# Attention with a soft mixture of experts on one core: the opening's roundings and duplicates reordered, logits spread ahead of the experts, extra constant products late

## Chip, core and metric

The kernel runs on one core of a Trainium2 chip. The core has five engines with a queue of their own each: PE (matrix products, into PSUM), DVE (vector), ACT (scalar functions and copies), POOL (general purpose) and SP, which here only issues transfers (DMA). Engines wait for each other by semaphores; each executes its own queue in order. The metric is the device time of one execution in microseconds.

## The reference

```python
def _attn_ref(q, k, v, f):            # q, k, v: 8 x 8 x 576 x 64; f: 8 x 8 x 576
    scale = 1.0 / np.sqrt(D)
    scores = scale * np.matmul(q, k.transpose(0, 1, 3, 2))
    cum = np.cumsum(np.log(np.clip(f, 0.0001, 1.0)), axis=-1)
    decay = cum[:, :, :, None] - cum[:, :, None, :]
    scores = np.where(causal, -1000000000.0, scores + decay)
    scores = scores - np.max(scores, axis=-1, keepdims=True)
    attn = np.exp(scores)
    attn = attn / (np.sum(attn, axis=-1, keepdims=True) + 1e-09)
    return np.matmul(attn, v)

def _moe_ref(x, phi, w1, w2):         # x: 4608 x 512; phi: 512 x 32; 8 experts, 4 slots each
    logits = x @ phi
    d = softmax over tokens of logits;  slot_input = d.T @ x
    for e in range(E):
        slot_out[e] = np.maximum(slot_input[e] @ w1[e], 0.0) @ w2[e]
    c = softmax over slots of logits
    return c @ slot_out
```

The attention's output, with heads side by side, is the x of the mixture.

## The kernel before

The 64 (batch, head) pairs are treated as 32 head pairs g, heads i = 2g and 2g + 1. For each head PE runs three stages. `s1` (L230) computes rough scores, whose row maxima DVE takes in `tops` (L243). PE turns these maxima (`mturn`, L253), ACT rounds them into a row (`mrows`, L262) and a transfer puts it into YA as one more contraction row. `s2` (L280, L281) computes the scores again, transposed and exactly, with the decay and minus the maximum in extra rows; the two products use the rounded operands WA, YA and a second pair WB, YB, which hold a duplicate of the rounded half and the difference that rounding left. ACT takes the exponential (`expo`, L287) into PTS, POOL zeroes the non-causal part (`causal`, L295, L298), and `s3` (L313) multiplies with the values V. DVE divides (`norm`, L328 to L333).

Operands are made as follows. `load_qk` loads a pair into one of three buffers RAW; `round_k` (L183) and `round_q` (L188) round it on ACT into WA and YA, a head at a time; `dup_k` (L199) and `dup_q` (L203) copy that by transfer into WB and YB; `low_k` (L209) and `low_q` (L214) subtract on POOL, which needs the duplicate (for k) or the rounded half (for q). `load_cum` brings the decay rows. All transfers are issued by SP, in program order.

The loop over g from 1 to 31 is a software pipeline: iteration g does `s2` and `s3` of pair g, `s1` of heads 2g + 3 and 2g + 4, and the roundings of pair g + 3. What comes ahead of it (pair 0, and the start of pairs 1 and 2) is written out by hand at L530 to L688 and is called the opening here. There the decay is made from f: logarithm (L558), prefix sum (L562), rounding (L571), rounding error (L572, L573); three copies on ACT (L583, L584) and transfers (L580) put these rows into WA[0] and WA[1]. The constant rows of WA and YA of the buffers 1 and 2 come from a small buffer `fill` by transfers (L575, L576). `warm` (L527) issues products of constants whose result nobody reads.

The order of everything is the order of the program; no scheduler moves instructions.

From iteration 5 on the mixture joins: logits (L387), a running maximum over tokens (`mgroup`, `mtop`, `mcast`), exponentials (`weigh2`), their transposes (`tokens`, L457, L458) and the sum over tokens (`dispatch`, L490). The logits of a batch come as 128 whole columns and 16 more for the last 64 tokens, which `spread` (L402) puts into a masked form LX with the help of `own_j` (L671, L672). After iteration 31 comes a tail (L858 to L910) for the last batch, with transposes of the combine weights (`cols`, L712) between its steps. Then the experts run from the list `STEPS`: first products (`mlp1`, L932), scaling and maximum with zero (`relu`, L940, L942), transposes of the hidden rows (`own`, L952, with copies at L955) and second products (`mlp2`, L969), with weights that are streamed (L128) into every buffer that has become free. The output blocks (L1047) are copied (L1049) and stored (L1051).

## Time and profile before

| | |
|---|---|
| time, three runs | 390.32, 390.36 and 391.53 us; median 390.36 us |
| the profiled execution's own time | 391.48 us |
| its span, first to last instruction | 389.8 us |
| mean granted clock of PE | 0.982 |
| busiest engines | PE 95%, DVE 76%, ACT 69%, POOL 65% of the span |
| start of `s2` of head 0, 2, 4, 6, 8 | 13.57, 26.82, 36.89, 45.66, 54.43 us |
| last weight transfer issued; first output issued | 351.6; 360.85 us |

A row of the order in time reads: start in us, duration in us, engine, line of the kernel, operation, what is written and read with its shape, count, and in brackets how long the engine idled before it and what ended that. A row of a stretch reads: from and to in us, its length, then busy time and instructions of PE, PE's weight loads, DVE, ACT and POOL, the clock granted to PE (1.00 is full), the mean busy share of the DMA engines and GB/s. A row of the chain reads: start, duration, what the end of the program waited for at that time.

### The profile page before, as it was taken

The numbers are of one execution on the slowest core, as the hardware profiler recorded it, in microseconds if no ns is written. First come the engines' busy times: TensorE is split into PE (matmuls) and PEld (weight loads), VectorE is DVE, ScalarE is ACT, GpSimd is POOL, SyncE is SP. The second block draws the span as 40 slices with busy tenths as digits, with TensorE's granted clock in tenths as the row PEclk, the third lists the DMA queues.
The fourth block names the chain that finished last, engine by engine and source line by source line (L and its number), as shares of the span: only waits on it lengthen the run. The fifth ranks groups of instructions, "written<-read, shape, count | busy, mean of one in ns | idle before, by whom it ended". The sixth has DMA issues, their size and how long they took to land.

```text
span 389.8 us, 15241 instructions
## 1 busy us (share of the span) xinstructions
PE 370.1 (95%) x5881; PEld 327.9 (84%) x5881; DVE 297.5 (76%) x1161; ACT 269.9 (69%) x685; POOL 251.6 (65%) x339
## 2 busy tenths in 40 slices
PE   8989999999999999999999999999999999999950
PEld 7879999999999999999999999999999986444630
DVE  7788887989798979897988898889988743412651
ACT  8887787878787878788878787878776553010540
POOL 3769987878787878787878787878787620000000
PEclk9999999999999999999999999999999998999995
DMA  6866667777867787777777777767765999999898
GB/s 206 230 153 161 172 189 208 200 199 243 243 197 224 216 236 218 218 209 216 215 211 215 215 213 213 220 208 220 211 183 159 309 341 385 409 408 373 270 358 345
DMA packets 34120, 93.72 MB, mean 240 GB/s; under 512 B 4234, under 2 KB 10048, under 8 KB 34048
## 3 DMA queue, kind: packets, MB, share of 16 engines
q1 hardware_dynamic: 34048, 92.75, 76.2%
q8 instruction: 46, 0.75, 0.8%
q14 instruction: 26, 0.21, 0.1%
HBM read 63.93 MB, written 9.73 MB: 189 GB/s over the span
## 4 chain that ended last, share of the span: by engine, by line
PE 79%; DMA 11%; POOL 3%; ACT 3%; DVE 2%; issue 1%; DVEq 0%; SPq 0%; ACTq 0%; POOLq 0%
PE pv L313 25%; PE ring L280 14%; PE ring L281 12%; PE s L230 11%; DMA w<-in_w 7%; PE pv L340 4%; PE lg L387 2%; PE ds L490 2%; POOL YB L214 1%; DMA out<-p 1%; DMA RAW<-in_qk 1%; PE pv L969 1%; PE ring L490 1%; ACT PTS L287 1%; DMA out<-RAW 1%
## 5 line engine op out<-in xcount | busy, mean ns | idle before, releaser
L287 ACT ACTIVATE PTS<-ring 128x320 f32<-128x320 f32 (+2 forms) x256 | 118.1, 502 | 50.2 <-PE ring L281 39.8
L243 DVE CUSTOM_DVE_ANT_0 s<-s,mask 128x320 f32<-128x320 f32 (+4 forms) x320 | 138.5, 452 | 6.1 <-PE s L230 1.0
L280 PE MATMUL ring<-YA,WA 67*128 67x320 f32 (+9 forms) x384 | 119.5, 325 | 0.0
L281 PE MATMUL ring<-YB,WB 128*128 128x320 f32 (+4 forms) x384 | 110.7, 296 | 0.0
L313 PE MATMUL pv<-V,PTS 128*64 128x65 f32 x3200 | 101.9, 223 | 0.9 <-POOL PTS L295 0.5
L209 POOL TENSOR_TENSOR WB<-RAW,WB 64x576 fp32r<-64x576 f32 x64 | 91.0, 1423 | 15.9 <-DMA YA<-V 5.3
L313 PEld LDWEIGHTS pv<-V,PTS 128*64 128x64 f32 x3200 | 97.1, 138 | 4.7 <-issue 1.2
L230 PE MATMUL s<-WA,YA 66*128 66x288 f32 (+9 forms) x384 | 100.4, 317 | 0.4 <-DVE MT L243 0.3
L214 POOL TENSOR_TENSOR YB<-RAW,YA 64x576 fp32r<-64x576 f32 x64 | 89.7, 1420 | 2.5
L280 PEld LDWEIGHTS ring<-YA,WA 67*128 67x128 f32 (+3 forms) x384 | 68.9, 181 | 5.3 <-issue 1.6
L281 PEld LDWEIGHTS ring<-YB,WB 128*128 128x128 f32 (+1 forms) x384 | 69.9, 182 | 0.0
L230 PEld LDWEIGHTS s<-WA,YA 66*128 66x128 f32 (+1 forms) x384 | 63.0, 191 | 5.3 <-DVE MT L243 0.5
L243 DVE DVE_READ_ACCUMULATOR2_ANT MT<- 128x1 f32 x372 | 52.7, 142 | 0.0
L298 POOL TENSOR_SCALAR_AFFINE_SELECT PTS<-PTS 128x128 f32<-128x128 f32 (+1 forms) x128 | 31.3, 265 | 29.9 <-ACT PTS L287 26.4
L295 POOL TENSOR_SCALAR_AFFINE_SELECT PTS<-PTS 128x384 f32<-128x384 f32 x64 | 33.3, 520 | 18.2 <-ACT PTS L287 14.1
L183 ACT CAST WA<-RAW 64x576 fp32r<-64x576 f32 x64 | 40.0, 669 | 4.0 <-DMA RAW<-in_qk 3.4
L340 PE MATMUL pv<-cs,X 128*128 128x128 f32 x155 | 42.1, 273 | 0.6 <-DVE X L333 0.6
L188 ACT CAST YA<-RAW 64x576 fp32r<-64x576 f32 x64 | 40.0, 669 | 0.4
L243 DVE CUSTOM_DVE_ANT_0 s<-s,mask,MT 128x288 f32<-128x288 f32 x62 | 32.6, 526 | 9.6 <-PE s L230 1.0
L333 DVE TENSOR_TENSOR X<-pv,rl 128x320 f32<-128x320 f32 (+1 forms) x65 | 31.5, 486 | 2.4 <-DMA V<-in_v 0.3
L376 ACT COPY XTS<-pv 128x128 f32<-128x128 f32 (+1 forms) x93 | 25.3, 307 | 1.1 <-PE pv L340 0.8
L340 PEld LDWEIGHTS pv<-cs,X 128*128 128x128 f32 x155 | 21.9, 142 | 1.5 <-DVE X L333 0.9
(215 smaller groups left out, 376.5 us busy)
## 6 DMA issues: line engine op xcount, KB each, us to landing
w<-in_w SPq DMA_DIRECT2D x44, 512.0 KB
RAW<-in_qk SPq DMA_DIRECT2D x31, 576.0 KB
V<-in_v SPq DMA_DIRECT2D x32, 325.0 KB
WB<-WA SPq DMA_DIRECT2D x31, 288.0 KB
YB<-YA SPq DMA_DIRECT2D x31, 288.0 KB
p<-in_w SPq DMA_DIRECT2D x7, 512.0 KB
out<-RAW SPq DMA_DIRECT2D x12, 256.0 KB
out<-p SPq DMA_DIRECT2D x5, 512.0 KB
```

Source lines behind the costliest of these rows:

```text
L183: nc.scalar.copy(WA[g % 3][0:64, S * h : S * h + S], RAW[g % 3][64:128, h])
L188: nc.scalar.copy(YA[g % 3][0:64, h, 64:640], RAW[g % 3][0:64, h])
L209: nc.gpsimd.tensor_tensor(t[0:64], RAW[g % 3][64:128, h], t[64:128].bitcast(F32), op=ALU.subtract)
L214: nc.gpsimd.tensor_tensor(YB[g % 2][64:128, h], RAW[g % 3][0:64, h], YA[g % 3][0:64, h, 64:640].bitcast(F32), op=ALU.subtract)
L230: nc.tensor.matmul(t[:, o : o + w], ya[0:m, h, 128 * blk : 128 * blk + 128], wa[0:m, j0 : j0 + w], start=True, stop=True)
L243: nc.vector.tensor_tensor_reduce(out=t[:, o : o + w], in0=t[:, o : o + w], in1=mask[:, m0 : m0 + w], scale=1.0, scalar=top if n == 3 else ...
L280: nc.tensor.matmul(o, wa[0:m, j0 : j0 + n], ya[0:m, h, 64 + i0 : 64 + i0 + w], start=True, stop=False)
L281: nc.tensor.matmul(o, wb[:, j0 : j0 + n], yb[:, h, i0 : i0 + w], start=False, stop=True)
L287: nc.scalar.activation(PT[i % 2][:, SEG_O[bank] : SEG_O[bank] + at], t[:, 0:at], AF.Exp, scale=0.125)
L295: nc.gpsimd.affine_select(d3, d3, pattern=[[0, 3], [1, 128]], compare_op=ALU.is_ge, fill=0.0, base=0, channel_multiplier=-1)
L313: nc.tensor.matmul(pvv[h][64 * u : 64 * u + 64, t, :], PT[h][:, at : at + 64], V[:, g % 2, c, 65 * h : 65 * h + 65], start=(c == 0), stop= ...
L340: nc.tensor.transpose(pm[:, 0:128], x[:, t, 128 * (p % 2) : 128 * (p % 2) + 128], ident)
```

## The change

Four things are changed.

1. The opening. The duplicates of pair 1 and 2 are issued by head, and their roundings come earlier or later, by head too. Two of the three ACT copies of decay rows become transfers, and the fill transfers are spread differently over the queue. The fill buffer lies in XTS instead of V. Score products of heads 1 to 4 (`first`) are moved among the values products and into iteration 1. Three warm products fewer are issued.
2. `own_j` is computed at the end of iteration 2 instead of in the opening.
3. In the tail five warm products of 64 or 128 columns are added, into a free part of the buffer pv[0].
4. In the experts, the logits of the last batch are copied and spread ahead of the first product instead of after the second expert's, and the last `own` is called one step earlier.

```diff
+    def fills(m, n):
+        if n == 0:
+            nc.sync.dma_start(WA[m][66:67].bitcast(F32), fill[0:1, 0 : 2 * S].bitcast(F32))
+        else:
+            nc.sync.dma_start(YA[m][64:66].rearrange("c h s -> c (h s)").bitcast(F32), fill[32:34].bitcast(F32))
+
     nc.vector.tensor_copy(fp[lane, 0:S], fz)
+    nc.sync.dma_start(WA[0][64:65, S:].bitcast(F32), fp[96:97, 0:S].bitcast(F32))
+    dup_k(0, 1, 2)
+    fills(1, 0)
...
-    for h in range(2):
-        nc.scalar.copy(WA[0][64:65, S * h : S * h + S], fp[64 + 32 * h : 65 + 32 * h, 0:S])
-    nc.scalar.copy(WA[0][96:97, S:], fp[96:97, S:])
+    nc.sync.dma_start(WA[0][96:97, S:].bitcast(F32), fp[96:97, S:].bitcast(F32))
...
+    fills(1, 1)
+    nc.scalar.copy(WA[0][64:65, 0:S], fp[64:65, 0:S])
     round_q(0, 1)
-    nc.scalar.activation(fin[:, 0:1], ones[:, 0:1], AF.Exp)
     dup_q(0, 1, 2)
...
     round_k(1, 0)
+    round_q(1, 0)
+    dup_k(1, 0, 1)
+    dup_q(1, 0, 1)
...
+    round_k(1, 1)
+    first(1, 3, WARM[1])
     both(0, 0)
-    first(1, 3)
+    first(2, 0)
     both(0, 1)
+    round_q(1, 1)
+    dup_k(1, 1, 2)
+    dup_q(1, 1, 2)
...
-    round_q(2)
-    first(3, 2)
-    first(3, 3)
+    round_k(2, 0)
+    round_q(2, 0)
+    dup_q(2, 0, 1)
+    dup_k(2, 0, 1)
     causal(1)
-    low_q(2)
     low_k(3)
     low_q(3)
-    nc.vector.tensor_reduce(own_j[:, 0], ident.rearrange("p (j s) -> p j s", j=4), axis=AX.X, op=ALU.add)
-    nc.vector.tensor_scalar(own_j[:, 1], own_j[:, 0], 1.0e30, -1.0e30, op0=ALU.mult, op1=ALU.add)
-    s3(0, alone[0])
+    s3(0, alone[0][:13])
+    first(3, 2)
+    s3(0, alone[0][13:])
+    first(3, 3)
+    s3(0, alone[1][:13])
     first(4, 0)
+    s3(0, alone[1][13:])
     mturn(1, 1, 2)
     mrows(1, 1, 2)
-    dup_q(2)
-    dup_k(2)
+    round_k(2, 1)
+    round_q(2, 1)
+    dup_q(2, 1, 2)
+    dup_k(2, 1, 2)
     first(4, 1)
...
-    round_k(3)
-    round_q(3)
...
         expo(h0, 2)
+        if g == 1:
+            round_k(3, 0)
+            round_q(3, 0)
...
+    warm(2, cs, 128, late=True)
     nc.vector.tensor_reduce(mb[:, 2:3], EX[:, 0:192], axis=AX.X, op=ALU.add)
...
     nc.vector.tensor_scalar_mul(mk, mk, fin[:, 2:3])
+    weigh(b)
+    spread(b, 0)
...
-        if (e, k) in ((2, 0), (4, 0), (6, 0), (5, 4)):
-            own({2: 0, 4: 2, 6: 4, 5: 6}[e])
+        if (e, k) in ((2, 0), (4, 0), (6, 0), (4, 4)):
+            own({(2, 0): 0, (4, 0): 2, (6, 0): 4, (4, 4): 6}[e, k])
         if (e, k) == (1, 0):
-            weigh(b)
-            spread(b, 0)
             tokens(b, 0)
             combine(b, 0)
```

The numbers behind names in the next rows are buffer numbers: RAW_95, RAW_96 and RAW_97 hold pairs 0, 1 and 2 (RAW_95 then pair 3), WA_86, YA_85, WB_88 and YB_87 belong to pair 1, WA_94 and YA_93 to pair 2.

SP's queue, from the load of pair 2 to the maxima row of head 2, before:

```order
L203 DMA YB_91<-YA_89 64x576
L174 DMA RAW_97<-in_qk 128x1152
L178 DMA V<-in_v 128x650
L174 DMA RAW_95<-in_qk 128x1152
L199 DMA WB_88<-WA_86 64x1152
L203 DMA YB_87<-YA_85 64x2x576
L194 DMA WA_94<-cumd 2x2x576
L265 DMA YA_85<-mr_0_337 1x5x128
```

and with the change:

```order
L174 DMA RAW_97<-in_qk 128x1152
L178 DMA V<-in_v 128x650
L199 DMA WB_88<-WA_86 64x576
L203 DMA YB_87<-YA_85 64x576
L199 DMA WB_88<-WA_86 64x576
L203 DMA YB_87<-YA_85 64x576
L194 DMA WA_94<-cumd 2x2x576
L265 DMA YA_85<-mr_0_336 1x5x128
L174 DMA RAW_95<-in_qk 128x1152
```

The duplicates of pair 1 are cut in two and stand ahead of the load of pair 3, which moves behind the maxima row.

ACT's queue from the first maxima row of pair 1 into iteration 1, before:

```order
L262 CAST mr_0_337<-pv_147 5x128
L183 CAST WA_94<-RAW_97 64x576 x2
L287 ACTIVATE PTS<-ring_150 128x320
L287 ACTIVATE PTS<-ring_151 128x512
L188 CAST YA_93<-RAW_97 64x576 x2
L262 CAST mr_1_408<-pv_148 5x128
L183 CAST WA_90<-RAW_95 64x576 x2
L188 CAST YA_89<-RAW_95 64x576 x2
L287 ACTIVATE PTS<-ring_149 128x448
L287 ACTIVATE PTS<-ring_150 128x320
L287 ACTIVATE PTS<-ring_151 128x320
```

and with the change, from the second maxima row on:

```order
L262 CAST mr_1_430<-pv_148 5x128
L183 CAST WA_94<-RAW_97 64x576
L188 CAST YA_93<-RAW_97 64x576
L287 ACTIVATE PTS<-ring_149 128x448
L287 ACTIVATE PTS<-ring_150 128x320
L287 ACTIVATE PTS<-ring_151 128x320
L183 CAST WA_90<-RAW_95 64x576
L188 CAST YA_89<-RAW_95 64x576
L376 COPY XTS<-pv_147 128x128 x2
L287 ACTIVATE PTS<-ring_149 128x512
L287 ACTIVATE PTS<-ring_150 128x448
L183 CAST WA_90<-RAW_95 64x576
```

Two roundings of pair 2 and all four of pair 3 now stand behind the second maxima row, those of pair 3 among the exponentials of iteration 1.

POOL's queue around the selection of head 1, the stretch that iteration 1 waits for, before:

```order
L209 TENSOR_TENSOR WB_88<-RAW_96,WB_88 64x576
L295 AFFINE_SELECT PTS<-PTS 128x3x128
L298 AFFINE_SELECT PTS<-PTS 128x128
L298 AFFINE_SELECT PTS<-PTS 128x64
L214 TENSOR_TENSOR YB_87<-RAW_96,YA_85 64x576
```

and with the change:

```order
L209 TENSOR_TENSOR WB_88<-RAW_96,WB_88 64x576
L214 TENSOR_TENSOR YB_87<-RAW_96,YA_85 64x576
L295 AFFINE_SELECT PTS<-PTS 128x3x128
L298 AFFINE_SELECT PTS<-PTS 128x128
L298 AFFINE_SELECT PTS<-PTS 128x64
```

The selection of head 1 moves behind the second subtraction of head 2.

In the tail the five warm products stand on PE behind the first two transposes of `cols`, ahead of the products of `mcast`, ahead of `tokens`, and two behind it:

```diff
     next(c0)
+    warm(1, cs, 64, late=True)
     mgroup(b)
...
     next(c0)
+    warm(1, cs, 64, late=True)
     mcast(b)
...
     next(c1)
+    warm(1, cs, 128, late=True)
     tokens(b, 1)
+    warm(2, cs, 128, late=True)
```

## Prediction

> **What bounds the kernel now.** I read the page first, then the chain of waits over the opening, then the stretches, then the opening and the end in order of time.

> ```profile
> span 389.8 us, 15241 instructions
> PE 370.1 (95%) x5881; PEld 327.9 (84%) x5881; DVE 297.5 (76%) x1161; ACT 269.9 (69%) x685; POOL 251.6 (65%) x339
> ...
> 34.42 0.53 POOL PTS L295
> 34.95 0.04 issue
> 35.00 1.96 PE pv L313 x58
> 36.96 0.40 PE ring L280
> ...
> 40.00:50.00 10.00, 9.97 (x152) 9.44 (x151) 8.36 (x36) 8.47 (x22) 8.51 (x13) 1.00 0.64 186
> ```

> PE is the engine of the long middle: from 40 to 50 us it is busy 9.97 of 10. What moves the start of that middle moves the end by as much. The first 37 us are different: in the chain PE's values product (L313) waits for POOL's causal selection (L295). Why POOL is late, the rows in order of time say:

> ```profile
> 5.81 0.52 SPq L199 DMA_DIRECT2D WB<-WA  x1
> 9.83 1.41 POOL L209 TENSOR_TENSOR WB<-RAW,WB 64x576 fp32r<-64x576 f32 x1 [5.31 <-DMA YA<-V]
> 17.26 0.67 ACT L183 CAST WA<-RAW 64x576 fp32r<-64x576 f32 x1
> 17.95 0.67 ACT L188 CAST YA<-RAW 64x576 fp32r<-64x576 f32 x1
> 17.96 0.48 SPq L199 DMA_DIRECT2D WB<-WA  x1
> 22.16 1.40 POOL L209 TENSOR_TENSOR WB<-RAW,WB 64x576 fp32r<-64x576 f32 x1 [5.12 <-DMA YB<-YA]
> 24.68 1.41 POOL L214 TENSOR_TENSOR YB<-RAW,YA 64x576 fp32r<-64x576 f32 x1
> ```

> The second pair's rounding ends on ACT at 17.9, its duplicate (both heads in one transfer) is issued at 17.96, and POOL's subtraction for head 2 starts at 22.16, after 5.12 us of idling: 4.2 us from issue to use. (The row names another buffer's transfer; the subtraction reads WB.) From 22.16 on POOL runs without a gap up to the selection of 34.42. So the opening costs PE whatever POOL is late.

> **The opening, step by step.** Roundings of both operands of head 2 move ahead of the first maxima on ACT, and the duplicate goes by head. The SP queue now fixes its time. Ahead of the first V load stand two issues more than before (the rows that ACT copied, now transfers):

> ```profile
> 7.10 0.59 SPq L575 DMA_DIRECT2D WA<-V  x1
> 13.88 0.33 SPq L178 DMA_DIRECT2D V<-in_v  x1
> ```

> An issue of this kind takes 0.59, so V goes out between 13.88 (if the queue's waits absorb the two) and 15.1; the duplicate of head 2 follows 0.33 later, 14.2 to 15.4. I take 15.0. It runs behind the same kind of load as before, so the 4.2 from issue to use stays: POOL starts at T = 19.2 instead of 22.16. Bounds: 14.2 + 4.0 (the first duplicate: issued 5.81, used 9.83) = 18.2, and 15.4 + 4.2 + 0.8 (more data ahead: both loads) = 20.4.

> POOL gains 3.0, but not all of it reaches PE, since the order behind it changes too. The selection of head 1 now stands behind both subtractions of head 2: 1.40 + 1.41 + 0.53 and issue gaps, so T + 3.45 = 22.65. Behind it PE has the values of head 1 in two halves with a score product between, then the turn of head 3's maxima (L253), and only then ACT's L262 can start. ACT is in order, and behind that L262 now stand six roundings that were done earlier or beside waits:

> ```profile
> 23.79 0.25 ACT L262 CAST mr<-pv 5x128 fp32r<-5x128 f32 x1 [0.17 <-PE pv L253]
> 25.97 0.92 PE L313 MATMUL pv<-V,PTS 128*64 128x65 f32 x24
> 27.53 1.31 ACT L287 ACTIVATE PTS<-ring 128x448 f32<-128x448 f32 x3 [0.95 <-PE ring L281]
> 29.68 0.43 ACT L376 COPY XTS<-pv 128x128 f32<-128x128 f32 x2 [0.84 <-PE pv L340]
> 30.75 1.03 ACT L287 ACTIVATE PTS<-ring 128x512 f32<-128x512 f32 x2 [0.64 <-PE ring L281]
> 31.67 0.38 ACT L376 COPY XTS<-pv 128x256 f32<-128x256 f32 x1
> 31.92 0.44 ACT L349 COPY XTS<-pv 64x64 f32<-64x64 f32 x2
> 32.38 0.77 ACT L287 ACTIVATE PTS<-ring 128x320 f32<-128x320 f32 x2
> 33.41 0.60 ACT L287 ACTIVATE PTS<-ring 128x512 f32<-128x512 f32 x1
> ```

> PE: two halves at about 0.8 (24 records took 0.92 with their latency), 0.5 for score product and turn: L262 at T + 5.6 = 24.8. Before, ACT waited 0.95 + 0.84 + 0.64 in this stretch; now it does not wait. Its work up to the last exponential of head 3: L262 twice 0.5, six roundings at 0.69 (17.26 to 17.95) 4.1, exponentials 1.31 + 1.03 + 0.77 + 0.60 = 3.7, copies 0.43 + 0.69 (31.67 to 32.36) = 1.1; sum 9.4, so ACT ends it at 34.2 (before: 34.01, the same place). PE's values are then half done, instead of waiting for POOL; about 23 of 50 products need that last exponential. At the pace of the row (58 records in 1.96) their 46 records take 1.55. The next score stage (before: 36.96 less its latency, 36.89) starts at 35.8. **Opening: 1.1 us earlier.** With T at 18.2 it is 2.1, at 20.4 nothing.

> Costs taken as nothing, and what covers them:

> ```profile
> 10.38 0.53 PE L230 MATMUL s<-WA,YA 97*128 97x320 f32 x2
> 11.62 0.53 DVE L243 CUSTOM_DVE_ANT_0 s<-s,mask 128x320 f32<-128x320 f32 x1
> 44.67 0.17 DVE L328 TENSOR_SCALAR rl<-pv 128x5 f32<-128x5 f32 x1 [0.82 <-PE pv L313]
> 22.65 0.94 DVE L672 TENSOR_SCALAR own_j<-own_j 128x4 f32<-128x4 f32 x1
> ```

> Head 1's decay rows now come by transfer; its first product ran at 10.38, and DVE reaches it at 11.62, so the rows may be 0.9 later for free, and 1:1 beyond. The own_j pair (0.94 and some 0.3) goes to the end of iteration 2, into DVE's 0.82 of waiting there; 0.4 remains, which the next iteration's wait takes up. Three warm products fewer in the opening fill waits only. The fill in XTS instead of V has the same shape.

> **The end.** After the last attention PE's clock is halved for a while, and PE waits at three places:

> ```profile
> 324.00:326.00 2.00, 1.73 (x36) 1.73 (x40) 1.32 (x5) 0.52 (x2) 0.00 (x0) 0.59 1.02 381
> 326.00:328.00 2.00, 2.00 (x18) 1.05 (x10) 0.64 (x2) 0.37 (x1) 0.56 (x2) 0.55 1.02 418
> 360.00:362.00 2.00, 2.00 (x32) 1.28 (x32) 0.88 (x3) 0.81 (x3) 0.00 (x0) 1.00 0.11 45
> ...
> 11.21 1.10 PE L527 MATMUL pv<-cs 128*128 128x184 f32 x6
> 318.50 0.84 PE L490 MATMUL ring<-X,LD 128*32 128x128 f32 x24
> 319.96 0.64 PE L490 MATMUL ring<-X,LD 128*32 128x128 f32 x16
> 324.27 2.32 PE L490 MATMUL ring<-X,LD 128*32 128x128 f32 x40 [0.42 <-DVE LD L464]
> 332.93 0.41 PE L458 MATMUL ring<-cs,LGM 128*128 128x32 f32 x2 [0.62 <-DVE LGM L402]
> 355.60 1.93 PE L969 MATMUL ring<-w,X 128*32 128x256 f32 x32 [0.35 <-DVE X L955]
> 360.85 4.22 SPq L1051 DMA_DIRECT2D out<-RAW  x6
> ```

> Between these PE runs gapless, and the first output leaves at 360.85; the DMA share of 0.11 in 360 to 362 says that the transfers then wait for PE, not for weights. So PE's gains here count, up to the 1.8 us that DMA idles there.

> The spread ahead of the experts removes the wait of 0.62, and the earlier own(6) the 0.35: **minus 0.97**. Late is next: the same products, without a wait. The five late products are fp32 of 64 to 128 columns. Three calls of 184 took 1.10; by columns (512 in all) five cost 1.0, at a full 0.37 each 1.85. The last two lie in the 0.42 that PE waits for LD; the others stand on the chain of maximum, broadcast and exponential. **Plus 0.6** (up to 1.4).

> They can pay by the clock. Forty products took 2.32 at the halved clock; 24 and 16 took 0.84 and 0.64 at the full one: 0.84 lost there, and with the transposes behind about 1.1. The profiled execution took 391.48 us by its own time (389.8 span and 1.7 around it); the runs shown took 390.32, 390.36 and 391.53. Two values, 1.1 apart: I read it as this drop, present in some executions and absent in others, so the median of 390.36 holds none. [...]

> **The sum**, against the profiled execution: 391.48 − 1.1 (opening) − 0.97 (two waits) + 0.6 (late products) − 1.1 (clock kept) = 388.8; with the rounding of the terms 388.9. Against the median that is 1.5 less, since the median has the clock's 1.1 already.

> **Rivals.**
> *The clock still drops.* For it: the window before the drop was already filled to nine tenths by the profile's count, and five short products add little. Then 388.9 + 1.1 = 390.0. [...]
> *The opening gives nothing.* ACT has no reserve in my chain; 1.1 us of waits there (PE behind DVE's maxima) eat it. 388.9 + 1.1 = 390.0.
> *The opening gives all of POOL's 3.0.* If PE and ACT reach their places early enough, T decides: 388.9 − 1.9 = 387.0. Against it: ACT's sum.
> *Slower: the duplicate lands no earlier.* It is cut in two but stands behind two loads. In the new order PE's next stage stands at T + 16.6, so the opening loses from T = 20.3 on. At the old T of 22.2 it starts at 38.8: 391.48 + 1.9 − 0.97 + 0.6 − 1.1 = 391.9. Against it: it is issued some 3 us sooner.

> **How the numbers follow.** Forecast 0.43; clock drops 0.20; opening nothing 0.16; all of POOL 0.13; slower 0.08. The range takes in all but the slower one: 387.0 to 390.3 (390.0 and a little for the dearer late products). 0.3%, about what a measurement of this kernel can tell from no change, is 1.17 us: the borders are 389.19 and 391.53. Of the forecast's 0.43, some 0.35 lies under 389.19 (T up to 19.5); with the 0.13 and 0.01 of the clock's case that makes faster 0.49. Slower is its 0.08 and 0.01 of the second rival; the rest, 0.42, is the same.

> **What would show it.** POOL's subtraction for head 2 near 19.2 and not 22.16. ACT gapless from L262 of head 3 to the last exponential of head 3. The score stage of pair 2 at 35.8. No PE wait ahead of L458 and between the experts' second products; first output 0.4 earlier relative to the last attention product, and 1.5 where the clock holds. A granted clock of 1.00 in the stretch after the late products. It would be wrong first where T or ACT's sum is.

## The result: slower by 0.9%

| | before | changed |
|---|---|---|
| median (lowest to highest) | 390.94 us (390.32 to 400.96, 4 runs) | 394.47 us (393.99 to 395.13, 4 runs) |
| profiled execution, own time and span | 391.48, 389.8 us | 393.99, 392.3 us |
| start of the score stage of head 4 (first L280) | 36.89 us | 40.76 us |
| from the start of the last values product to the end of the span | 75.2 us | 73.7 us |

The ratio is 1.0086, interval 1.0061 to 1.0111: slower, where 388.9 and a range up to 390.3 were predicted. The 400.96 is an execution in a slower state, which the ratio leaves out; the other three have a median of 390.36. The last two rows of the table divide the loss. The opening gives head 4 to PE 3.9 us later, the middle passes that on, and the end wins 1.5 back: 3.9 − 1.5 = 2.4, as the two profiled executions differ (393.99 − 391.48 = 2.5). The end is as predicted (1.47); the opening is 5.0 later than the 35.8 of the prediction.

The page of the changed kernel begins:

```profile
span 392.3 us, 15255 instructions
PE 370.3 (94%) x5885; PEld 327.6 (84%) x5885; DVE 297.3 (76%) x1161; ACT 268.9 (69%) x683; POOL 252.2 (64%) x339
```

PE's busy time is the same as before (370.1), so nothing costly was added: in sum PE waits longer, though it may also compute slower in one place and faster in another. The chain of waits (start, duration, what the end waited for) leads there:

```profile
17.09 4.91 DMA YB<-YA
22.03 1.40 POOL YB L214
...
36.11 4.71 PE pv L313 x100
46.47 3.14 PE pv L313 x100
```

The values product of iteration 1 (36.11) takes 4.71 and the next one 3.14, and a transfer and POOL stand ahead. The same stretch in order of time, for SP, POOL, PE and ACT (start, duration, engine, line; in brackets how long the engine idled and what ended it):

```profile
14.25 0.39 SPq L174 DMA_DIRECT2D RAW<-in_qk  x1
14.69 0.43 SPq L178 DMA_DIRECT2D V<-in_v  x1
15.23 0.48 SPq L199 DMA_DIRECT2D WB<-WA  x1
20.56 1.41 POOL L209 TENSOR_TENSOR WB<-RAW,WB 64x576 fp32r<-64x576 f32 x1 [2.76 <-DMA WB<-WA]
24.08 1.26 PE L313 MATMUL pv<-V,PTS 128*64 128x65 f32 x26 [0.97 <-POOL PTS L295]
26.56 0.27 PE L253 MATMUL pv<-cs,MT 128*5 128x128 f32 x1
26.91 0.26 ACT L262 CAST mr<-pv 5x128 fp32r<-5x128 f32 x1 [4.59 <-PE pv L253]
28.60 0.40 PE L230 MATMUL s<-WA,YA 66*128 66x288 f32 x1 [1.08 <-ACT YA L188]
33.20 0.67 ACT L183 CAST WA<-RAW 64x576 fp32r<-64x576 f32 x1
33.88 0.67 ACT L188 CAST YA<-RAW 64x576 fp32r<-64x576 f32 x1
35.17 0.77 ACT L287 ACTIVATE PTS<-ring 128x320 f32<-128x320 f32 x2
35.82 0.24 ACT L262 CAST mr<-pv 10x128 fp32r<-10x128 f32 x1
35.97 0.58 ACT L287 ACTIVATE PTS<-ring 128x512 f32<-128x512 f32 x1
36.11 4.71 PE L313 MATMUL pv<-V,PTS 128*64 128x65 f32 x100 [1.52 <-ACT mr L262]
40.76 0.47 PE L280 MATMUL ring<-YA,WA 67*128 67x448 f32 x1
```

Four things differ from the prediction. POOL starts at T = 20.56, not 19.2. ACT idles 4.59 and reaches the maxima row (L262) of head 3 at 26.91, where it was at 23.79 before. The values product waits 1.52, not for POOL and not for its own exponentials, but for the *next* maxima row, the second L262. Both use the buffer pv[0], though different columns of it: the product writes columns 0 to 324, the turned maxima lie in 325 to 452. The first 21 of the product's 50 values need only head 2, whose exponentials end at 33.17 and whose selection ends at 33.3; the product starts 0.05 behind the end of L262 (35.82 + 0.24). Between the two maxima rows ACT's queue now holds six roundings where it held four. And the product then runs slowly. The stretches (from, to, length, busy us and instructions of PE, PE's loads, DVE, ACT, POOL, granted clock, DMA share, GB/s) show how:

```profile
34.00:36.00 2.00, 0.59 (x7) 0.46 (x5) 1.93 (x10) 1.96 (x8) 0.80 (x1) 1.00 0.31 122
36.00:38.00 2.00, 1.89 (x36) 1.89 (x38) 0.12 (x2) 1.96 (x5) 1.82 (x4) 0.56 0.01 3
38.00:40.00 2.00, 2.00 (x48) 2.00 (x46) 0.31 (x2) 1.07 (x2) 1.93 (x2) 0.59 0.61 120
...
326.00:328.00 2.00, 2.00 (x23) 1.51 (x21) 0.85 (x5) 1.14 (x4) 0.00 (x0) 1.00 0.99 317
```

After a stretch in which PE worked 0.59 of 2 us, its clock is halved (what the runs show of that is in the last section); the trace's record of the granted clock has it from 36.23 for 3.413 us. In the end of the program the clock now stays at 1.00, and the two waits are gone: L458 follows without an idle time.

```profile
335.86 0.31 PE L458 MATMUL ring<-cs,LGM 128*128 128x32 f32 x2
```

### The profile page after: what moved, and what is told of

It reads as the page before. It is cut to its first block, busy times and chain, and to the rows that moved or that the text cites. A ratio compares the mean times of both kernels' runs of the same rounds, so it can differ in the third digit from the quotient of the medians.

```text
span 392.3 us, 15255 instructions
## 1 busy us (share of the span) xinstructions
PE 370.3 (94%) x5885; PEld 327.6 (84%) x5885; DVE 297.3 (76%) x1161; ACT 268.9 (69%) x683; POOL 252.2 (64%) x339
## 4 chain that ended last, share of the span: by engine, by line
PE 87%; DMA 4%; ACT 3%; SPq 1%; issue 1%; DVE 1%; POOL 0%; DVEq 0%; ACTq 0%; POOLq 0%
PE pv L313 26%; PE ring L280 14%; PE ring L281 12%; PE s L230 11%; PE pv L340 4%; PE pv L991 3%; PE lg L387 2%; PE ds L490 2%; PE ring L954 2%; PE pv L954 2%; DMA YB<-YA 2%; DMA out<-p 1%; PE ring L991 1%; PE pv L253 1%; DMA out<-RAW 1%
## 5 line engine op out<-in xcount | busy, mean ns | idle before, releaser
L287 ACT ACTIVATE PTS<-ring 128x320 f32<-128x320 f32 (+2 forms) x256 | 118.4, 502 | 50.9 <-PE ring L281 38.9
L243 DVE CUSTOM_DVE_ANT_0 s<-s,mask 128x448 f32<-128x448 f32 (+4 forms) x320 | 138.4, 452 | 8.2 <-PE s L230 3.0
L280 PE MATMUL ring<-YA,WA 67*128 67x320 f32 (+9 forms) x384 | 119.5, 324 | 0.1
L281 PE MATMUL ring<-YB,WB 128*128 128x320 f32 (+4 forms) x384 | 110.8, 296 | 0.0
L313 PE MATMUL pv<-V,PTS 128*64 128x65 f32 x3200 | 103.4, 225 | 2.8 <-ACT mr L262 1.5
L313 PEld LDWEIGHTS pv<-V,PTS 128*64 128x64 f32 x3200 | 98.5, 139 | 6.5 <-ACT mr L262 2.4
L230 PE MATMUL s<-WA,YA 66*128 66x288 f32 (+9 forms) x384 | 100.7, 317 | 2.0 <-ACT YA L188 1.1
L209 POOL TENSOR_TENSOR WB<-RAW,WB 64x576 fp32r<-64x576 f32 x64 | 91.1, 1424 | 13.6 <-DMA WB<-WA 8.4
L214 POOL TENSOR_TENSOR YB<-RAW,YA 64x576 fp32r<-64x576 f32 x64 | 89.7, 1420 | 2.4
L280 PEld LDWEIGHTS ring<-YA,WA 67*128 67x128 f32 (+3 forms) x384 | 68.9, 181 | 5.7 <-issue 1.6
L281 PEld LDWEIGHTS ring<-YB,WB 128*128 128x128 f32 (+1 forms) x384 | 69.9, 182 | 0.0
L230 PEld LDWEIGHTS s<-WA,YA 66*128 66x128 f32 (+1 forms) x384 | 63.2, 191 | 7.4 <-ACT YA L188 1.4
L243 DVE DVE_READ_ACCUMULATOR2_ANT MT<- 128x1 f32 x372 | 52.5, 141 | 0.0
L295 POOL TENSOR_SCALAR_AFFINE_SELECT PTS<-PTS 128x384 f32<-128x384 f32 x64 | 33.5, 523 | 21.5 <-ACT PTS L287 16.3
L183 ACT CAST WA<-RAW 64x576 fp32r<-64x576 f32 x64 | 40.2, 669 | 3.6 <-DMA RAW<-in_qk 2.8
L340 PE MATMUL pv<-cs,X 128*128 128x128 f32 x155 | 42.1, 273 | 0.0
L243 DVE CUSTOM_DVE_ANT_0 s<-s,mask,MT 128x288 f32<-128x288 f32 x62 | 32.6, 525 | 10.9 <-PE s L230 2.7
L188 ACT CAST YA<-RAW 64x576 fp32r<-64x576 f32 x64 | 40.2, 669 | 0.4
L376 ACT COPY XTS<-pv 128x128 f32<-128x128 f32 (+1 forms) x93 | 25.2, 306 | 0.3
L328 DVE TENSOR_SCALAR rl<-pv 128x5 f32<-128x5 f32 x64 | 10.2, 160 | 16.5 <-PE pv L313 14.4
```

The source lines that it names most:

```text
L183: nc.scalar.copy(WA[g % 3][0:64, S * h : S * h + S], RAW[g % 3][64:128, h])
L188: nc.scalar.copy(YA[g % 3][0:64, h, 64:640], RAW[g % 3][0:64, h])
L209: nc.gpsimd.tensor_tensor(t[0:64], RAW[g % 3][64:128, h], t[64:128].bitcast(F32), op=ALU.subtract)
L214: nc.gpsimd.tensor_tensor(YB[g % 2][64:128, h], RAW[g % 3][0:64, h], YA[g % 3][0:64, h, 64:640].bitcast(F32), op=ALU.subtract)
L230: nc.tensor.matmul(t[:, o : o + w], ya[0:m, h, 128 * blk : 128 * blk + 128], wa[0:m, j0 : j0 + w], start=True, stop=True)
L243: nc.vector.tensor_tensor_reduce(out=t[:, o : o + w], in0=t[:, o : o + w], in1=mask[:, m0 : m0 + w], scale=1.0, scalar=top if n == 3 else ...
```

## The experiments

The kernel before was run beside each group: 391.42 us for the first four runs, 391.22 for the next, 390.68 for the last (31, 19 and 35 runs). Where an expectation names 38.13 for head 4 in the run with the roundings early, the row has 38.56.

### Which part loses: the end alone, the opening alone

The first run is the kernel before with parts 3 and 4 of the change, these lines; the second is the changed kernel without them.

```diff
+    warm(1, cs, 64, late=True)
     mgroup(b)
...
     tokens(b, 1)
+    warm(2, cs, 128, late=True)
...
+    weigh(b)
+    spread(b, 0)
...
-        if (e, k) in ((2, 0), (4, 0), (6, 0), (5, 4)):
+        if (e, k) in ((2, 0), (4, 0), (6, 0), (4, 4)):
```

> The kernel before with the change's tail alone (five late products, logits spread ahead of the experts, own one step earlier). Theory A (the opening's order lost the time, the end won): from the end of the last values product to the end of the program the changed kernel was 1.6 us shorter than before, so 391.48 - 1.6 = 389.9 us by the profiled execution, and PE's granted clock stays 1.00 in the tail. Rival C (the late products cost more than they bring): 391 us or more.

> The change's opening alone, with the end as before. Theory A: the score stage of pair 2's successor (head 4) starts at 40.9 us as in the changed kernel (before: 36.9), so about 4 us over the kernel before: 394.4 to 395.5 us. Rival C: no slower than before, about 390 to 391 us.

| | median | ratio |
|---|---|---|
| end alone | 389.85 us | 0.9950 [0.9917, 0.9984] |
| opening alone | 394.11 us | 1.0082 [1.0052, 1.0112] |

The end gains and the whole loss is the opening's. Added up, the two make 0.3%, less than the 0.9% of the change; that lies at the edge of what their intervals allow. In the traces of the two kernels the parts do add up (3.9 − 1.5 against 2.5). The profiled execution of the opening alone lost more clock than that of the change: head 4 starts at 42.04 in it, not at the 40.9 expected.

### The wait for the maxima row, and the clock

One run rounds head 6 on ACT in the 4.59 us in which it idled; the other leaves everything and fills PE's wait with three products of constants.

```diff
 # roundings early
+    round_k(2, 1); round_q(2, 1); round_k(3, 0); round_q(3, 0)
     mturn(1, 1, 2)
     mrows(1, 1, 2)
-    round_k(2, 1); round_q(2, 1)
...
 # wait filled
+        if g == 1:
+            warm(3, cs)
         s3(g, VALUES[:29])
```

> The changed kernel, with four roundings (pair 2's second head, pair 3's first head) put on ACT ahead of the second maxima row, where ACT idled 4.6 us. Theory A (the six roundings behind that row make the next maxima row late, and PE's values product of iteration 1 waits for that): ACT's L262 of iteration 1 about 2.7 us earlier (33.1 instead of 35.8), values product from about 34.7 at the latest, no clock drop there: 390.9 to 391.5 us. Rival B (the later transfers bound the opening: duplicate used at 20.6, loads behind it): no gain, 394.0 us.

> The changed kernel with three constant products on PE ahead of the values product of iteration 1, where PE idles 1.5 us. Theory A: half of the loss behind the wait is the clock, halved from 36.3 to 39.8; with PE filled it stays at 1.00 and the values product takes 3.2 instead of 4.7 us: 392.6 us. If the fill doesn't decide the clock: 394.0 us, or up to 0.5 more.

PE and ACT in order of time, roundings early, then PE with the wait filled:

```profile
35.20 0.24 ACT L262 CAST mr<-pv 10x128 fp32r<-10x128 f32 x1
35.49 3.14 PE L313 MATMUL pv<-V,PTS 128*64 128x65 f32 x100 [1.19 <-ACT mr L262]
38.56 0.47 PE L280 MATMUL ring<-YA,WA 67*128 67x448 f32 x1
```

```profile
35.18 1.20 PE L527 MATMUL pv<-cs 128*128 128x184 f32 x6 [0.59 <-ACT XTS L349]
36.31 3.13 PE L313 MATMUL pv<-V,PTS 128*64 128x65 f32 x100
39.38 0.47 PE L280 MATMUL ring<-YA,WA 67*128 67x448 f32 x1
```

The filled wait leaves the start of the values nearly where it was (36.31 against 36.11) and their duration falls from 4.71 to 3.13, with the clock at 1.00: the half clock cost 1.4 us at head 4, with nothing else changed in that stretch. With the roundings early L262 is 0.62 earlier, where 2.7 had been expected: with four roundings out of the way ACT waits for PE's products instead (1.17 at 29.33, then 0.68 and 0.64). The values product is 0.62 earlier too, at 0.29 behind the start of L262 as in the change; it runs at full clock (1.00 from 34 to 40), and head 4 comes 2.2 earlier. In the medians this is 392.23 us (1.0038 [1.0009, 1.0068]), still slower than before, and for the fill 393.61 (1.0072 [1.0040, 1.0104]), hardly better than the change. With the fill the clock holds in some executions only: five of its ten took 392.0 to 392.9 us at a mean clock of 0.983 to 0.987, five 394.3 to 396.3 at 0.971 to 0.977. The opening alone, without a fill, had a mean clock of 0.985 in three of its ten, so it isn't shown that the fill is what kept it here. Filling one wait doesn't settle it. The stretch ahead of it is thin as a whole, as one row over 14 us shows, first of the kernel before, then of the changed one:

```profile
22.00:36.00 14.00, 12.83 (x203) 11.48 (x200) 11.49 (x50) 11.10 (x26) 13.23 (x17) 1.00 0.54 142
```

```profile
22.00:36.00 14.00, 10.53 (x117) 8.94 (x113) 10.71 (x49) 8.58 (x22) 10.37 (x12) 1.00 0.60 178
```

PE is busy 10.53 of 14 us where it was 12.83.

The next run goes further: the roundings of head 7 stand behind the second maxima row.

```diff
         expo(h1, 0)
-        if g == 1:
-            round_k(3, 1)
-            round_q(3, 1)
...
         mrows(g + 1)
+        if g == 1:
+            round_k(3, 1)
+            round_q(3, 1)
```

> As the run with the roundings of head 6 early, and in addition the two roundings of head 7 on ACT stand behind the second maxima row of iteration 1 instead of ahead of it. Theory (the values product of iteration 1 waits for that maxima row, L262, and not for its own exponentials): L262 of 10x128 at 33.9 to 34.4 instead of 35.20, the wait of 1.19 ahead of L313 falls to 0.3 or less, score stage of head 4 at 37.1 to 37.4 instead of 38.13, 391.2 to 391.5 us. Rival (the last exponentials of head 3 set the place, with ACT's sum unchanged): the wait moves into the middle of L313, head 4 at 38.1, 392.2 us.

```profile
33.89 0.24 ACT L262 CAST mr<-pv 10x128 fp32r<-10x128 f32 x1
34.34 3.33 PE L313 MATMUL pv<-V,PTS 128*64 128x65 f32 x100
37.61 0.47 PE L280 MATMUL ring<-YA,WA 67*128 67x448 f32 x1
```

The wait is gone and head 4 is 0.95 earlier than in the run before it, as the theory had it. The time wasn't: 393.66 us (1.0063 [1.0038, 1.0088]). The profiled execution is the fastest of five (391.81 us, mean clock 0.987); the others took 392.8 to 395.5 at 0.972 to 0.976. The order of the opening leaves the clock at risk, even where its waits are shortened. (This edit brings the exponentials ahead of L262 forward as well; what tells the two apart is the order of the values and the 0.05 above.)

### What POOL's start is worth

Here the duplicates of head 2 go out ahead of the loads, on top of the early roundings.

```diff
     dup_q(0, 1, 2)
+    nc.scalar.activation(fin[:, 0:1], ones[:, 0:1], AF.Exp)
+    round_k(1, 0); round_q(1, 0)
+    dup_k(1, 0, 1); dup_q(1, 0, 1)
     nc.sync.dma_start(cumd...)
     fills(2, 0)
     fills(2, 1)
     load_qk(2)
     load_v(0)
...
```

> As the run with the roundings of head 6 early, and in addition the two duplicates of head 2 are issued ahead of the decay rows, the fill rows of buffer 2 and the loads of pair 2 and of V. Theory (POOL's start T is late because the duplicate stands behind two loads in the DMA engines): issued near 12, landed before 17, POOL starts its subtraction for head 2 as soon as it is free, at about 17.8 instead of 20.6; PE's wait of about 1 us for the selection of head 1 goes; the score stage of head 4 1.0 earlier than 38.13, 391.2 us. Rival 1 (a duplicate needs some 5 us wherever it stands): T not under 19.5, half of it or less. Rival 2 (T comes early, but PE and ACT have no gap to close): T at 17.8 and head 4 within 0.3 of 38.13, 392.2 us.

POOL, PE and ACT in order of time:

```profile
18.48 1.41 POOL L209 TENSOR_TENSOR WB<-RAW,WB 64x576 fp32r<-64x576 f32 x1
20.26 0.24 ACT L262 CAST mr<-pv 5x128 fp32r<-5x128 f32 x1
23.82 1.26 PE L313 MATMUL pv<-V,PTS 128*64 128x65 f32 x26
26.30 0.27 PE L253 MATMUL pv<-cs,MT 128*5 128x128 f32 x1
26.73 0.25 ACT L262 CAST mr<-pv 5x128 fp32r<-5x128 f32 x1
```

POOL now starts at 18.48 without idling, 2.1 earlier, and PE's wait of 0.97 is gone. The maxima row of head 3 comes at 26.73, where the changed kernel has it at 26.91. That looks like rival 2, but this execution was late on PE before it came here: a score product waits 0.83 up to 11.48, where the changed kernel has 0.22 up to 10.88, and the first maxima row stands at 20.26 instead of 19.65. (The run with all four moves issues these duplicates as early and has that row at 19.65, so the delay seems to be this execution's.) Without these 0.6 the row of head 3 would come near 26.1, by estimate. So POOL's start is worth some 0.8 there; the other 2.3 against the 23.79 of before are the work that PE has queued ahead of the turn (L253). In this execution the clock was halved from near 31.3 on for some 6.8 us (0.82 over 30 to 32, 0.50 up to 38, 0.98 up to 40), so its head 4 (40.15) and its 393.28 us (1.0055 [1.0033, 1.0076]) say nothing more.

So PE's order was tested: the last score groups of head 3, and its turn, ahead of the values of head 1 again.

```diff
+    first(3, 2)
+    first(3, 3)
...
-    s3(0, alone[0][:13])
-    first(3, 2)
-    s3(0, alone[0][13:])
-    first(3, 3)
-    s3(0, alone[1][:13])
+    s3(0, alone[0])
     first(4, 0)
-    s3(0, alone[1][13:])
     mturn(1, 1, 2)
     mrows(1, 1, 2)
+    s3(0, alone[1])
```

> The changed kernel with one move: the last two score groups of head 3 and the turn of its maxima, with the row that ACT makes of it, stand on PE ahead of the values of head 1 again, as in the kernel before. Theory (what makes the maxima row of head 3 late is PE's own queue ahead of the turn, not POOL's start T): L262 of 5x128 at 23.8 to 24.2 instead of 26.91 with T unchanged near 20.5; PE's wait of 1.08 for the rounding of head 5 goes; ACT still has four roundings between the exponentials, so the score stage of head 4 comes at 37.6 to 38.9 instead of 40.87; 391.9 to 392.6 us. Rival (POOL's selection sets it): L262 earlier by the 0.97 that PE waits at most, head 4 not before 39.9, 393.5 us.

ACT in order of time:

```profile
23.29 0.25 ACT L262 CAST mr<-pv 5x128 fp32r<-5x128 f32 x1 [0.95 <-PE pv L253]
```

A stretch of the same profile:

```profile
30.00:32.00 2.00, 2.00 (x12) 1.76 (x11) 1.97 (x10) 1.52 (x4) 0.52 (x1) 0.57 0.91 357
```

The row comes 3.6 us earlier with POOL's start unchanged (20.33): the place of the turn in PE's queue set it, behind the values that wait for POOL. But head 4 at 39.58 and 393.0 us (1.0066 [1.0027, 1.0106]) miss the expected 37.6 to 38.9, since the clock is halved from near 30.3 on for some 6.8 us (0.57 over 30 to 32, 0.50 up to 36, 0.72 up to 38).

All four moves together:

> The changed kernel with all four moves together: the turn of head 3's maxima early, the duplicates of head 2 ahead of the loads, the roundings of head 6 early and those of head 7 behind the maxima row of iteration 1. Theory (these are the causes of the loss): T 18.5, first L262 near 24, the second at 33.0 to 33.5, values product gapless from 33.4, no half clock in the opening, score stage of head 4 at 36.4 to 36.7; 389.9 to 390.2 us, like the kernel before with the tail's waits removed. Rival (the order of the score products leaves PE thin and the clock drops whatever ACT does): head 4 past 37.5 in the profile or times over 392 us.

```profile
33.28 0.24 ACT L262 CAST mr<-pv 10x128 fp32r<-10x128 f32 x1
33.71 3.35 PE L313 MATMUL pv<-V,PTS 128*64 128x65 f32 x100
37.00 0.47 PE L280 MATMUL ring<-YA,WA 67*128 67x448 f32 x1
```

391.08 us, 1.0009 [0.9977, 1.0040]: these four moves take the loss against the kernel before away. Against the end alone (389.85 us, ratio 0.9950, in another group) 1 to 2 us remain. Head 4 stands 0.3 past what was expected (the values product takes 3.35, with ACT's roundings now ahead of its last exponential), and three of ten executions still took 393.1 to 394.3 us at a clock of 0.969 to 0.975, as the rival has it; the other seven have a median of 390.35. No gain is left of the opening, though the end's 1.5 us is in this kernel.

### The end, taken apart, and the best version

The two waits alone, and the five late products alone, each on the kernel before:

> The kernel before with the logits spread ahead of the experts and the earlier call of own, without the late products. Theory (the two waits of 0.62 and 0.35 go, and the half clock in the tail comes from the transposes and stays): 0.9 to 1.0 under the kernel before, clock halved for 3.41 us near 324 in the profile. Rival (the waits are worth nothing, what the tail part brings is the clock): no difference.

> The kernel before with the five late products alone. Theory (the products cost 0.6 on the path and keep the clock at full, worth 1.1 where it dropped): no half clock near 324 in the profile, time 0.5 under the kernel before where that drops its clock and 0.6 over it where it doesn't, so within 0.5 of it. Rival (they are idle ballast): the half clock stays near 324 and the time is 0.6 over.

The waits alone give 390.05 us, 0.9968 [0.9955, 0.9981]. There is no half clock in the end of that profile (1.00 from 316 to 338), though it has the transposes and no late product. Nor is there one in the profile of the opening alone, whose end is that of the kernel before: it takes 74.5 us from the start of the last values product, where the kernel before with its drop takes 75.2. So the drop is a matter of the execution, and cost some 0.7 by these two profiles. The late products alone give 392.43 us, 1.0030 [1.0011, 1.0050]. The profiled execution of that run was disturbed in the opening, as is told below, but not in its end: that takes 74.4 us at full clock (1.00 from 316 to 338), against the 74.5 with the same two waits and no late product. The pair that prices them in the medians is built on a new opening: the order of before, with the duplicates of pair 1 by head, the second subtraction of head 2 ahead of the selection of head 1, and at the end the two waits removed. Of this the diff shows the opening.

```diff
     dup_q(0, 1, 2)
+    round_k(1, 0)
+    dup_k(1, 0, 1)
     load_qk(2)
     load_v(0)
...
     round_q(1, 0)
+    dup_q(1, 0, 1)
...
-    dup_k(1)
-    dup_q(1)
+    dup_k(1, 1, 2)
+    dup_q(1, 1, 2)
...
     low_k(2)
+    low_q(2)
...
     causal(1)
-    low_q(2)
```

> The kernel before with the two waits at the end removed (as in the run with the waits only) and, of the opening's changes, one alone: the duplicates of pair 1 by head, that of head 2's k issued ahead of the load of pair 2, and both subtractions of head 2 ahead of the selection of head 1. Theory (POOL's lateness is all that this can mend, and PE's stage ahead of the values ends at 33.3): T near 17.1 instead of 22.16, the values product gapless from 33.3, score stage of head 4 at 36.4 to 36.5 instead of 36.9; 0.4 under the waits alone, 389.6 us. Rival (another wait takes its place): head 4 at 36.9 and 390.05 us. The prediction's sum would have it at 35.8.

> The run with the duplicates by head, and the five late products beside it. The pair of runs prices the late products. The prediction's term: 0.6 dearer where the clock holds without them, 0.5 cheaper where it would drop. Rival 1 (ballast): 0.6 dearer in every execution, whatever the clock. Rival 2 (they lie in PE's waits): within 0.2 of the run without them.

POOL and PE in order of time, duplicates by head:

```profile
17.35 1.41 POOL L209 TENSOR_TENSOR WB<-RAW,WB 64x576 fp32r<-64x576 f32 x1
33.23 3.14 PE L313 MATMUL pv<-V,PTS 128*64 128x65 f32 x100
36.29 0.47 PE L280 MATMUL ring<-YA,WA 67*128 67x448 f32 x1
```

389.62 us, 0.9960 [0.9940, 0.9980], with twelve executions between 389.2 and 389.85: the best version found, 0.4% under the kernel before and 1.2% under the changed one. POOL starts 4.8 us earlier than before, and head 4 comes 0.6 earlier, no more: PE's stage ahead of the values ends at 33.2 (33.3 before), and only the wait inside the product goes. (Two other profiles with the opening of before have head 4 at 36.72 and 37.08, so the 0.6 is 0.4 to 0.8.) Most of the gain in time is that of the two waits, 0.9968 by themselves. With the late products beside it 389.77 us, 0.9965 [0.9942, 0.9987], and from the start of the last values product to the end 73.3 us in both profiles (73.5 with the waits alone, 75.2 before): there the late products cost and bring nothing. The loss that they showed in the medians on the kernel before, alone, is explained neither by that pair nor by the end of its profile; it stays open.

## Why the prediction was wrong, step by step

- **T = 19.2** (bounds 18.2 to 20.4): 20.56. The term was "the 4.2 from issue to use stays". It was issued at 15.23, nearly as taken, but was used 5.3 later, behind the loads of pair 2 and V. Issued ahead of them it made POOL wait for nothing (18.48). A size, 1.4 us. The slower rival's own rule, head 4 at T + 16.6, gives only 37.2 for this T.
- **L262 at T + 5.6**: at T + 6.35 in the change, and T + 8.25 in the run with the duplicates first. This is a wrong model more than a size. The sum began at POOL and left out PE's own queue: the change moves head 3's last score groups among the values products and the turn behind all of them, so that the row can't come before some 26.1 (the estimate above), whatever POOL does. It was at 23.79 before, and at 23.29 with the turn put back ahead of the values.
- **ACT's 9.4 up to the last exponential of head 3**: 26.91 to 36.55 is 9.64. Right in size, but ACT wasn't gapless: it waited for PE twice, 0.35 and 0.33, so the two bound each other. With four roundings taken out, ACT's waits for PE ate most of the gain.
- **"PE's values are then half done"**: the step whose mechanism failed. The values product doesn't start when PE is free; it waits for the next maxima row on ACT, which now stands behind six roundings and nearly all exponentials. None of its values is done when the last exponential starts at 35.97. It begins whole at 36.11. In the kernel before the same pair stands 3 us earlier, ACT and PE in order of time:

```profile
33.03 0.24 ACT L262 CAST mr<-pv 10x128 fp32r<-10x128 f32 x1
33.09 0.22 PE L281 MATMUL ring<-YB,WB 128*64 128x64 f32 x1
33.33 1.50 PE L313 MATMUL pv<-V,PTS 128*64 128x65 f32 x42
```

  The product starts 0.30 behind the row in this profile too, but that shows nothing: PE has work up to 33.31 and doesn't wait. The dependence was to be read in the program, where `mturn` and `s3` use the same pv[0]. With the row out of the way by one step (35.20) the product followed it, by two (33.89) PE had no wait left.
- **The clock in the opening**: priced at nothing, without a reason, since no term named it. The prediction saw the half clock at the end and priced it there, but didn't ask whether the clock holds behind its own new waits (0.97, 1.08, 1.52). It measures 1.4 to 1.6 in the profile (by the run with the wait filled, and by 4.71 against 3.14), and in the profile of the opening alone the half clock lasts three times as long (some 10.2 us, by its stretches).
- **The sum for head 4**, 35.8 against 40.76: T 1.4, T to L262 0.75, ACT 0.25, the values behind L262 1.05, the clock 1.55 make 5.0.
- **The end, −0.97 + 0.6 − 1.1**: the total, −1.47, measures −1.5, but so close a match is luck: the nine profiles with the change's whole end spread from 72.9 to 73.8. The waits went as told: −1.0 in the profiles (74.5 to 73.5), −1.25 by the ratio of the waits alone, from −0.7 to −1.8. The late products cost nothing in the profiles (74.4 against 74.5, 73.3 against 73.3), where 0.6 was put down. The drop was worth some 0.7, where 1.1 was put down. That the late products keep the clock was the author's assumption, and no run shows this term: without them the end had no half clock in three profiles either. The two errors nearly cancel. The median of before, read as free of that drop because the runs shown took "two values, 1.1 apart", can't be told so: the 85 executions beside the experiments spread from 389.9 to 392.8 without a break between two such values, with seven above.
- **The total**: the terms as written give 388.91; the 388.8 ahead of "rounding" is a slip without effect.
- **Rivals.** The slower one rested on T alone, with 0.08 and 391.9 us; it did not hold the mechanism that came. The dependence of the values product on L262 would have given one: six roundings at 0.69 stand between the two maxima rows in the new order.

## What to carry to other kernels

When an instruction of one engine is moved, follow for each engine the *next* thing that waits on that queue, also through buffers that are shared without any data flowing: here a values product waited for a copy of the next pair's maxima. An earlier start of one engine is worth at most the time that the engine which it feeds really waits for it (some 0.6 us here, of 4.8 moved). Where PE is kept near full by hand, count its busy share in each stretch ahead of a long product: behind a thin one here (0.59 of 2 us) stood a wait of 1.52 and a half clock, and the product took 4.71, where it takes 3.13 at the full one; behind another (0.81 of 2 us, in the profile with the roundings early) the clock held.

## What the runs showed of the hardware

**The clock dropped without a long wait, and a busy PE didn't bring it back at once.** In the changed kernel PE was busy 1.89 of the 3.41 us ahead of the drop, with no wait over 1.52. Nor is it the busy time alone: the changed kernel kept the clock behind a stretch (25.99 to 29.40) in which PE was busy 2.33, and the opening alone lost it behind one (27.28 to 30.70) that was as busy, with 33 and 16 records of PE. In the run of the opening alone, PE's busy time was full and the clock stayed at half:

```profile
32.00:34.00 2.00, 2.00 (x10) 1.76 (x10) 1.37 (x7) 1.41 (x4) 0.62 (x3) 0.50 0.91 282
...
36.00:38.00 2.00, 2.00 (x20) 1.89 (x21) 1.61 (x7) 1.41 (x4) 0.52 (x1) 0.50 0.00 0
38.00:40.00 2.00, 2.00 (x44) 2.00 (x42) 0.23 (x2) 1.96 (x5) 1.77 (x3) 0.50 0.19 42
```

It came back near 40.9, behind a stretch in which the values product ran (some 22 records in a us), and not behind those with score products alone (5 in a us). The profile's busy time doesn't tell where the clock drops and where it comes back; what does isn't shown.

**One duplicate came 3 us late.** In the profiled execution of the late products alone, whose opening is that of the kernel before, POOL got the duplicate of head 2 at 25.13 instead of 22.16, after idling 7.73, though its work ahead of that ended within 0.4 us of before (17.40 and 17.05):

```profile
25.13 1.40 POOL L209 TENSOR_TENSOR WB<-RAW,WB 64x576 fp32r<-64x576 f32 x1 [7.73 <-DMA WB<-WA]
```

PE waited 3.15 us behind it, the clock was at 0.51 from 28 to 30 us (0.963 over the whole execution), and this execution took 400.2 us. In the 24 executions of the two kernels that issue this transfer ahead of the loads and keep the rest of the opening nearly as before none took over 390.6 us, while the kernel before, beside them, ranged to 396.06. That the transfer is the reason isn't shown: the five executions of the two waits alone, with the transfer where it was, took no more than 390.3 either.
